# Loading the first expert's weights: four blocks at once, or two, one and two more

## The chip, the cores and the metric

One core of one Trainium2 chip runs the whole program in one launch. The metric is the device time of one execution in microseconds (us), median of the timed runs. The engines of the core are TensorE (PE: matmuls and transposes; its weight loads are listed as PEld), VectorE (DVE), ScalarE (ACT), GpSimd (POOL) and SyncE (SP), which here only issues transfers. Sixteen DMA engines move the data.

## The reference

Three stages: attention with a block-causal mask over 32 heads of 576 tokens, a mixture of eight experts in which each of the 2304 tokens goes to the expert with the highest logit, and a two-layer network with a piecewise quadratic activation.

```
scores = where(mask, q @ k.T / 8, -1e9); attn = softmax(scores); x = attn @ v   # B, H, S, D = 4, 8, 576, 64
x = x as [2304, 512]
logits = x @ w_gate + modality_bias[modality_id]
e_idx = argmax(logits); gate_w = softmax(logits)[e_idx]
for e in range(8):                       # w1[e]: 512 x 1024, w2[e]: 1024 x 512
    h = maximum(x[e_idx == e] @ w1[e], 0)
    out[e_idx == e] = gate_w * (h @ w2[e])
h = out @ w_in                           # 512 x 2048
g = where(h >= 1, h, where(h <= -1, 0, (h + 1)**2 / 4))
result = g @ w_out                       # 2048 x 512
```

All is float32. The kernel keeps the accuracy by splitting operands into a high and a low part and adding three products.

## The kernel before

The program runs through attention (to about 218 us), the experts (to about 446) and the network. Every engine works in an order that is written out by the program's text.

**Attention** goes through 16 pairs of heads, each in seven steps (`scores`, `flip`, `soft`). The rows of x of a finished batch are written to DRAM by `rows` (the store is line 459). From pair 14 on the generator `early` (`Routing.first_slot`) finds the expert that most of the first 13 row tiles go to; when it is done, `weights.begin` is called (line 519), still inside attention.

**The weights** of an expert come in eight blocks f = 0 to 7 of 128 hidden units. A block is 128 columns of w1 and 128 rows of w2, two transfers of 256 KB on SyncE's queue (lines 566 and 568). There are four buffers (`NRAW`). `Weights.load(most)` issues blocks, in order, until `most` are held in `self.raw`; a block leaves `raw` when `convert` has made its low part.

**The experts** run as five slots of 512 tokens; slots 0 and 1 are for the expert that was found first. `run_slots` goes over the blocks (s, f), numbered z. In each, `convert(s, f, 0)` lets ScalarE cast a raw block to its high part `wh` (line 1100) two blocks ahead, and `convert(s, f, 1)` lets VectorE make the low part `wl` (line 1103) one block ahead, which frees the raw buffer. `first` multiplies by w1 (line 1019) and takes ReLU on ScalarE to `hh` and on VectorE to `hl`; `second` multiplies by w2 (line 1128). `gather` fetches a slot's rows by indirect transfers on GpSimd (line 1078); `turn` transposes 128 rows, and ScalarE and VectorE split them into `xhi` and `xlo` (lines 76 and 77).

**The seam** is the generator `begin`, which still has attention's last work to do. Its order: casts of block 0, row group 0 turned, the rest of the last pair, row group 1 turned, cast of block 1, three of the left rows of x (`tail.rows`), and, at u == 3, `weights.load()` and a `yield`. Then the loop of `run_slots` begins with z = 0: cast of block 2, low part of block 1, `weights.load()`, and the first half (256 columns) of the first h. Between its halves `first` lets `begin` go on: row groups 2 and 3 are turned and the remaining left rows are made. The second half of the first h needs these two row groups.

So before the change four blocks are issued at `weights.begin`, block 4 at the seam, block 5 in z = 0, block 6 in z = 1 and so on.

Of the kernel before, what the change touches and what calls it, by code (L numbers as in the profile page):

```python
# [39 lines left out]
NFIRST = 2  # L40
# [3 lines left out]
NRAW = 4  # L44
# [78 lines left out]
def attention(late, weights, tc, q, k, v, ids, w_gate, mbias, x_dram, dram, ident, tabs):  # L123
# [15 lines left out]
    def load_pair(n, names="qkv"):  # L139
        b, c = divmod(n, NP)  # L140

        queue = dict(q=nc.sync if n else nc.scalar, k=nc.sync, v=nc.sync)
        for nm, src in zip("kqv", (k, q, v)):
            if nm not in names:
                continue
            dt = F32 if nm == "v" or n < COPY else F32R
            x = (pvp if nm == "v" else io).tile([P, 5, P], dt, tag=nm, name=f"{nm}{n}", bufs=3)
            if nm == "v":
                for h in range(2):
                    nc.sync.dma_start(  # L150
                        out=x[:, :4, h * D:(h + 1) * D],
                        in_=src[b, 2 * c + h, :512, :].rearrange("(t p) d -> p t d", p=P))

                for p0, s0 in ((0, 512), (64, 448)):
                    nc.sync.dma_start(
                        out=x[p0:p0 + 64, 4, :].rearrange("p (h d) -> p h d", d=D),
                        in_=src[b, 2 * c:2 * c + 2, s0:s0 + 64, :].rearrange("h p d -> p h d"))
            else:

                part = copies.pop((n, nm)) if n >= COPY else src[b, 2 * c:2 * c + 2]  # L160
                for h in range(2):
                    hs = slice(h * D, (h + 1) * D)
                    queue[nm].dma_start(out=x[:, :3, hs].bitcast(F32),
                                        in_=part[h, :384, :].rearrange("(t p) d -> p t d", p=P))
                    queue[nm].dma_start(out=x[:, 3:, hs].bitcast(F32),
                                        in_=part[h, 320:, :].rearrange("(t p) d -> p t d", p=P))
            io_t[n, nm] = x
# [4 lines left out]
    def copy_pair(n):  # L172

        b, c = divmod(n, NP)
        for nm, src in zip("kq", (k, q)):
            t = dram.tile([2, S, D], F32, name=f"{nm}c{n}")
            flat = "h s d -> (h s d)"
            nc.sync.dma_start(out=t.rearrange(flat).rearrange("(p x) -> p x", p=P),
                              in_=src[b, 2 * c:2 * c + 2].rearrange(flat).rearrange("(p x) -> p x", p=P))
            copies[n, nm] = t  # L180
# [124 lines left out]
    def scores(n, i):  # L305
        if n not in nmaxs:
            nmaxs[n] = wk.tile([P, NB], F32, tag="nmax", name=f"nmax{n}")
        j, heads = kinds[i]
        qa, qb, qf = qas[n % 2], qbs[n % 2], qfs[n % 2]
        kT, kd, kl = qk[n]  # L310
        if j == 4:

            pss = ps2.tile([P, 1024], F32, tag="big", name=f"s{n}_{i}")[:, 512 - S // 2:512 + S // 2]
            for c0, c1 in ((0, S // 2), (S // 2, S)):
                for z, (a, b) in enumerate(((qa[:, 0, 6:8], kd[:, 0]), (qzs[n % 2], kd[:, 1]), (qb[:, 6:8], kl))):
                    nc.tensor.matmul(pss[:, c0:c1], a, b[:, c0:c1], start=(z == 0), stop=(z == 2))
            return pss
        w = P * (j + 1)
        pss = ps1.tile([P, 512], F32, tag="s", name=f"s{n}_{i}", bufs=SB)[:, :w * len(heads)]
        for u, h in enumerate(heads):  # L320
            us = slice(u * w, (u + 1) * w)
            if j == 0:
                nc.tensor.matmul(pss[:, us], qf[:, h], kT[:, :w], start=(u == 0), stop=False)
            else:
                x = slice(2 * j - 2, 2 * j)
                nc.tensor.matmul(pss[:, us], qa[:, h, x], kd[:, h, :w], start=(u == 0), stop=False)
                nc.tensor.matmul(pss[:, us], qb[:, x.start + 8 * h:x.stop + 8 * h], kl[:, :w], start=False, stop=False)
        u = len(heads)
        nc.tensor.matmul(pss.rearrange("p (u w) -> p u w", u=u)[:, :, w - 64:], maskq,
                         maskk[:, :64 * u], start=False, stop=True)  # L330
        return pss
# [137 lines left out]
    def act(n, z, at):  # L469

        if n >= B * NP:
            return
        for what in PLAN.get((z, at), ()):
            if what == "q" and n + 1 < B * NP:
                load_q(n + 1)
            elif what == "k" and n + 1 < B * NP:
                load_k(n + 1)
            elif what == "rows" and todo:
                done.add(todo[0])
                rows(*todo.pop(0))  # L480
            elif n == 0:
                continue
            elif isinstance(what, tuple):
                weigh(n - 1, *what)
            elif what == "sum" and (n - 1) % 2:
                row_sums((n - 1) // NP, (n - 1) % NP // 2)
            elif what == "first":
                weigh_first(n - 1)
            elif what == "store":
                store_xT(n - 1)  # L490
                if (n - 1) % 2:
                    todo.extend((j, (n - 1) % NP // 2) for j in rows_of[(n - 1) // NP])
# [5 lines left out]
    for g in range(len(steps) + LAG):  # L498
        n, z = divmod(g, NK)
        if z in (0, 1) and n + 2 < B * NP:  # L500
            load_pair(n + 2, "v" if z else "qk")
        if z == 3 and COPY <= n + 4 < B * NP:
            copy_pair(n + 4)
        act(n, z, 0)
        pss = scores(*steps[g]) if g < len(steps) else None
        act(n, z, 1)
        later = flip(*steps[g - LAG]) if g >= LAG else []
        if pss is not None:
            soft(*steps[g], pss)
        for dst, src in later:  # L510
            nc.vector.tensor_copy(dst, src)  # L511
        if n >= B * NP:
            continue

        if n >= 14:
            assert all((j, a) in done for j in range(NEARLY) for a in range(2))
            for _ in range(EARLY[1] if weights.raw else EARLY[0]):
                if next(early, None):
                    weights.begin(0, range(1, NFIRST))
        act(n, z, 2)  # L520
        if (n, z) == (1, 0):
            load_gate()
        if (n, z) == (6, 0):
            routing.constants()
            early = routing.first_slot(ps1)
        if n == 8 and z == 5:
            routing.prep(ids, mbias, ident, ps1)
# [425 lines left out]
def experts_and_mlp(ctx, bctx, late, tc, a_tail, weights, w_in, w_out, x_dram, y_dram, g_dram, out,  # L953
# [111 lines left out]
    def run_slots(slots, begin, between, part=0):  # L1065
# [83 lines left out]
        for z, (s, f) in enumerate(blocks):  # L1149
            nxt = s + 1 if s + 1 in slots else None  # L1150
            if f == 1 and nxt:
                gather(nxt)
            if z + CONV < len(blocks):
                convert(*blocks[z + CONV], 0)
            between(s, f, 0)
            if z + CONV - 1 < len(blocks):
                convert(*blocks[z + CONV - 1], 1)
            weights.load()
            between(s, f, 1)
            if (s, f) == (NSTAT - 1, NF - 2) and not part:  # L1160
                tc.mark_branch_hint_location("more", engines=ENGINES)

            first(s, f)
            between(s, f, 2)
            if z > 0:
                second(*blocks[z - 1])
            if f in TURNS and nxt:
                turn(nxt, TURNS.index(f))
            between(s, f, 3)
# [3 lines left out]
    def begin(turn, convert):  # L1173
        tail.row_sums()
        convert(0, 0, 0)
        convert(0, 0, 1)
        turn(0, 0)
        tail.weigh()
        tail.weigh_first()
        tail.store_xT()  # L1180
        turn(0, 1, True)
        convert(0, 1, 0)
        for u, (j, a) in enumerate(tail.left):
            if u in (3, 4, 6):
                xr = b_y.tile([P, DM], F32, tag="y", name=f"xrows{u}")
            if u == 3:
                weights.load()
                yield
                turn(0, 2)
                turn(0, 3, True)  # L1190
            tail.rows(j, a, u % 3 == 0, None if u < 3 else xr[:, u % 2 * 256:(u % 2 + 1) * 256])
        tail.ps2.close()
        tail.pv.close()
        tabs.late_pool = late.enter_context(tc.tile_pool(name="r_late", bufs=1, side="right"))
        tabs.psa = pool("psa", 4, space=PSUM, side="right")
# [385 lines left out]
```

## Time and profile before

| | |
|---|---|
| median of 3 runs | 840.74 us (840.67 to 841.1) |
| the profiled execution | 839.69 us |
| its span, first to last instruction | 837.8 us |
| mean granted TensorE clock | 0.992 |
| busy: PE, DVE, ACT, POOL | 98%, 73%, 59%, 25% of the span |

Times in the trace count from the span's start. An idle time in square brackets stands before an instruction, with what ended it. A line xN stands for N instructions one behind the other; its second number is then the time from the first start to the last end. The granted clock is 1.00 at 2.4 GHz and 0.50 at 1.2 GHz. The DMA share is the mean busy share of the 16 DMA engines. Matmuls are pipelined, and their ends are modelled.

### The profile page before, as it was taken

To read this page: it belongs to the slowest core of one execution; us is meant where nothing else is said; L and a number is where in the kernel's file an instruction comes from. 1 tells how busy PE (TensorE), PEld (TensorE's weight loads), DVE (VectorE), ACT (ScalarE), POOL (GpSimd) and SP (SyncE) were. 2 spreads that over 40 slices of the span, in tenths; PEclk is the share of its full clock that TensorE was granted. 3 is DMA by queue.
4 is the path that set the end of the run, shared out by engine and by line. 5 is a ranking of instruction groups with operands and counts; after the bars stand their busy time and mean duration, and the time that the engine had idled before them with its cause. 6 is when DMAs were issued, how large, how long until landed. Compare 5 with 4: busy or idle time off the path is not lost. (4 is left out here: it accounts for less than half of the span.)

```text
span 837.8 us, 13997 instructions
## 1 busy us (share of the span) xinstructions
PE 817.9 (98%) x4936; PEld 709.3 (85%) x4936; DVE 608.3 (73%) x1115; ACT 495.6 (59%) x994; POOL 205.4 (25%) x249
## 2 busy tenths in 40 slices
PE   6999999998899999999999999999999999999998
PEld 5777777775788888888888999999999988888887
DVE  6788888789666656797873766766636877777774
ACT  5898888896533334464544666766657644444442
POOL 8546556546301212120202000110000011112120
PEclk6999999999999999999999999999999999999999
DMA  6445655630744447765625453453644633333301
GB/s 155 119 125 144 172 145 134 171 95 20 247 131 150 153 125 234 240 204 163 203 84 162 142 176 121 170 175 134 218 120 160 239 143 128 125 126 126 132 32 38
DMA packets 138058, 123.17 MB, mean 147 GB/s; under 512 B 70183, under 2 KB 122423, under 8 KB 135296
## 3 DMA queue, kind: packets, MB, share of 16 engines
q1 hardware_dynamic: 132256, 107.98, 41.9%
q0 software_dynamic: 4384, 13.92, 4.7%
q8 instruction: 40, 0.66, 0.3%
q10 hardware_dynamic: 1344, 0.33, 0.2%
q14 instruction: 34, 0.28, 0.1%
HBM read 89.17 MB, written 40.37 MB: 155 GB/s over the span
## 5 line engine op out<-in xcount | busy, mean ns | idle before, releaser
L1019 PE MATMUL h<-yhi,wi 128*128 128x384 f32 x768 | 200.4, 338 | 1.1 <-ACTq L1253 1.1
L1019 PEld LDWEIGHTS h<-yhi,wi 128*128 128x128 f32 x768 | 139.5, 188 | 1.5 <-ACTq L1253 1.5
L1019 PE MATMUL h<-ylo,wi 128*128 128x384 f32 x384 | 129.2, 337 | 0.0
L1293 ACT ACTIVATE cl<-h,half 128x384 f32<-128x384 f32 x96 | 55.9, 582 | 69.4 <-PE h L1019 69.1
L350 ACT ACTIVATE pall<-s,nmax 128x384 f32<-128x384 f32 (+2 forms) x144 | 79.5, 558 | 28.1 <-DVE nmax L344 17.0
L1297 DVE SCALAR_TENSOR_TENSOR gg<-cl,h 128x384 f32<-128x384 f32 x96 | 52.3, 552 | 51.8 <-ACT cl L1294 49.7
L1423 PE MATMUL p<-wo,s 128*128 128x256 f32 (+1 forms) x432 | 87.8, 338 | 0.0
L1423 PEld LDWEIGHTS p<-wo,s 128*128 128x128 f32 x432 | 68.5, 188 | 9.2
L1478 POOL DMA_INDIRECT out_dram<-rest,tab x16 | 27.3, 1707 | 190.9 <-DVE rest L1445 185.4
L1019 PEld LDWEIGHTS h<-ylo,wi 128*128 128x128 f32 x384 | 72.1, 188 | 0.0
L368 PE MATMUL pt<-ident,pall 128*128 128x128 f32 x400 | 65.7, 282 | 5.5 <-DVE pT L511 3.5
L1423 PE MATMUL p<-wo,a 128*128 128x256 f32 (+1 forms) x330 | 66.0, 335 | 0.0
L1019 PE MATMUL h<-xhi,wh 128*128 128x512 f32 (+2 forms) x164 | 63.1, 385 | 0.0
L1019 PE MATMUL h<-xhi,wl 128*128 128x512 f32 (+2 forms) x164 | 61.7, 376 | 0.5 <-DVE wl L1103 0.5
L1019 PE MATMUL h<-xlo,wh 128*128 128x512 f32 (+2 forms) x164 | 61.6, 376 | 0.0
L1128 PE MATMUL acc<-wh,hl 128*128 128x512 f32 x152 | 59.6, 392 | 0.1
L1423 PEld LDWEIGHTS p<-wo,a 128*128 128x128 f32 x330 | 52.8, 188 | 7.9
L1128 PE MATMUL acc<-wl,hh 128*128 128x512 f32 x152 | 59.3, 390 | 0.0
L1128 PE MATMUL acc<-wh,hh 128*128 128x512 f32 x152 | 59.1, 389 | 0.0
L393 PE MATMUL px<-pT,v 128*64 128x448 f32 (+4 forms) x320 | 54.5, 432 | 0.0
L1294 ACT ACTIVATE cl<-cl 128x384 f32<-128x384 f32 x96 | 50.5, 526 | 3.0
L368 PEld LDWEIGHTS pt<-ident,pall 128*128 128x128 f32 x400 | 43.9, 143 | 7.0 <-issue 3.1
(316 smaller groups left out, 1807.8 us busy)
## 6 DMA issues: line engine op xcount, KB each, us to landing
raw<-in_moe_w_dram SPq DMA_DIRECT2D x80, 256.0 KB
g_dram<-gg SPq DMA_DIRECT2D x48, 384.0 KB
g<-g_dram SPq DMA_DIRECT2D x18, 1024.0 KB
wi_raw<-in_moe_w_in_dram SPq DMA_DIRECT2D x16, 512.0 KB
wo_raw<-in_moe_w_out_dram SPq DMA_DIRECT2D x16, 512.0 KB
yr<-y_dram SPq DMA_DIRECT2D x18, 256.0 KB
x_dram<-xrow SPq DMA_DIRECT2D x33, 128.0 KB
v<-in_v_dram SPq DMA_DIRECT2D x32, 128.0 KB
```

The costliest lines, as they stand in the source:

```text
L350: nc.scalar.activation(pall[n % 2][:, o:o + w], pss[:, u:u + w], AF.Exp, bias=nm[:, x:x + 1], scale=1.0, accum_out=ssum[:, b, c, x:x + 1])
L368: nc.tensor.transpose(pt[:, kk, :], pa[:, o + kk * P:o + (kk + 1) * P], ident)
L393: nc.tensor.matmul(pxs[n][h * 64:(h + 1) * 64, s0 - 64:], io_t[n, "v"][:, kk, h * D:(h + 1) * D], pTs[n][:, kk, h, s0:], start=(kk == 0), ...
L1019: nc.tensor.matmul(ps, a[za], b[zb], start=(i == 0), stop=(i == n - 1))
L1128: nc.tensor.matmul(accs[s][u], a[:, us], b[:, 1, :], start=(f == 0 and i == 0), stop=(f == NF - 1 and i == 2))
L1293: nc.scalar.activation(cl, ph, AF.Relu, bias=half, scale=0.5)
L1294: nc.scalar.activation(cl, cl, AF.Square)
L1297: nc.vector.scalar_tensor_tensor(gg[:, :, f % 2, :], cl.rearrange(t3, t=P), 1.0, ph.rearrange(t3, t=P), op0=ALU.min, op1=ALU.max)
L1423: nc.tensor.matmul(o, a, b, start=(x == 0 and i in FRESH), stop=(x == len(terms) - 1), skip_group_check=True)
L1478: outs.append(nc.gpsimd.indirect_dma_start(out=out[:, :], out_offset=bass.IndirectOffsetOnAxis(ap=tabs.tab[:, j, 0:1].bitcast(U32), axis=0 ...
```

## The change

`weights.begin` loads two blocks instead of four. The load at the seam fills up to two held blocks; at that place block 0 has been released and block 1 has not, so it issues one block, block 2. The load in step z of the loop fills up to 3 + z blocks, at most four: in z = 0 blocks 3 and 4, in z = 1 blocks 5 and 6, and from z = 2 one block a step as before.

```diff
@@ -516,7 +516,7 @@
             for _ in range(EARLY[1] if weights.raw else EARLY[0]):
                 if next(early, None):
-                    weights.begin(0, range(1, NFIRST))
+                    weights.begin(0, range(1, NFIRST), 2)
         act(n, z, 2)
@@ -1155,7 +1155,7 @@
             if z + CONV - 1 < len(blocks):
                 convert(*blocks[z + CONV - 1], 1)
-            weights.load()
+            weights.load(min(NRAW, 3 + z))
             between(s, f, 1)
@@ -1184,7 +1184,7 @@
             if u == 3:
-                weights.load()
+                weights.load(2)
                 yield
```

`run_slots` serves further slots too, behind a branch; in the trace of before there are 40 blocks, five slots of eight, so that branch is not taken.

## Rows read from the trace of the kernel before

**Rows 1.** The page: span, busy time by engine, the chain that ended last.
```profile
span 837.8 us, 13997 instructions
...
PE 817.9 (98%) x4936; PEld 709.3 (85%) x4936; DVE 608.3 (73%) x1115; ACT 495.6 (59%) x994; POOL 205.4 (25%) x249
...
PE h L1019 24%; PE p L1423 21%; PE yt L1059 1%; PE p L1427 0%; DVE rest L1440 0%; DVEq L1440 0%
```

**Rows 2.** What PE waited for, 219 to 445: total us, times, longest.
```profile
PE h L1019 <- DVE wl L1103: 0.5, 2, 0.2
```

**Rows 3.** Busy us by engine in stretches of the seam; clock, DMA share, GB/s.
```profile
212.00:214.50 2.50, 2.50 (x27) 1.98 (x25) 0.55 (x3) 1.83 (x5) 1.89 (x3) 1.00 1.06 308
214.50:218.00 3.50, 0.93 (x6) 0.61 (x5) 1.73 (x4) 1.80 (x6) 1.14 (x2) 1.00 0.97 309
218.00:223.00 5.00, 4.84 (x39) 3.91 (x40) 3.47 (x11) 2.98 (x8) 0.94 (x1) 1.00 0.94 321
...
226.50:230.50 4.00, 3.99 (x31) 3.69 (x30) 3.02 (x9) 1.50 (x3) 1.98 (x2) 1.00 0.88 273
```

**Rows 4.** Timeline of PE at the stop: start, us, instruction [idle before it].
```profile
215.82 0.33 PE L368 MATMUL pt<-ident,pall 128*128 128x128 f32 x1 [1.22 <-issue]
...
218.13 0.84 PE L368 MATMUL pt<-ident,pall 128*128 128x128 f32 x6 [1.49 <-DVE pT L511]
```

**Rows 5.** Timeline of DVE at the stop.
```profile
215.24 0.43 DVE L344 TENSOR_REDUCE nmax<-s 128x2 f32<-128x256 f32 x1 [2.66 <-PE pt L368]
```

**Rows 6.** Timeline of SyncE's queue at the seam (the issues, not the transfers).
```profile
210.33 0.41 SPq L566 DMA_DIRECT2D raw<-in_moe_w_dram  x1
...
214.48 0.84 SPq L568 DMA_DIRECT2D raw<-in_moe_w_dram  x1
...
226.49 0.39 SPq L566 DMA_DIRECT2D raw<-in_moe_w_dram  x1
227.10 0.39 SPq L568 DMA_DIRECT2D raw<-in_moe_w_dram  x1
...
229.15 1.34 SPq L459 DMA_DIRECT2D x_dram<-xrows  x3
```

**Rows 7.** Timeline of ACT at the seam.
```profile
223.67 2.02 ACT L1100 CAST wh<-raw 128x1024 fp32r<-128x1024 f32 x2
226.49 1.07 ACT L76 CAST xhi<-xt 128x512 fp32r<-128x512 f32 x2 [0.80 <-PE xt L1093]
230.07 0.60 ACT L1116 ACTIVATE hh<-h 128x512 fp32r<-128x512 f32 x1 [2.50 <-PE h L1019]
230.56 1.04 ACT L1100 CAST wh<-raw 128x1024 fp32r<-128x1024 f32 x1
```

**Rows 8.** Timeline of PE: the second half of the first h, its first xlo product.
```profile
228.45 0.38 PE L1019 MATMUL h<-xlo,wh 128*128 128x256 f32 x1
```

**Rows 9.** Timeline of DVE: the low parts of row groups 2 and 3.
```profile
227.11 1.29 DVE L77 TENSOR_TENSOR xlo<-xt,xhi 128x512 fp32r<-128x512 f32 x2 [0.17 <-issue]
```

**Rows 10.** Timeline of SyncE's queue: a block's first issue, later in slot 0.
```profile
251.55 0.38 SPq L566 DMA_DIRECT2D raw<-in_moe_w_dram  x1
```

**Rows 11.** Stretches around that block; the last two numbers are DMA share, GB/s.
```profile
251.50:252.50 1.00, 1.00 (x7) 0.80 (x6) 1.00 (x2) 0.31 (x1) 0.00 (x0) 1.00 0.00 0
252.50:254.50 2.00, 2.00 (x13) 1.69 (x12) 1.46 (x3) 1.53 (x2) 0.00 (x0) 1.00 0.81 259
254.50:255.50 1.00, 1.00 (x6) 0.83 (x5) 0.84 (x1) 0.00 (x0) 0.00 (x0) 1.00 0.02 6
```

**Rows 12.** Stretches at the start of the run; the granted clock stands before DMA share.
```profile
5.00:10.00 5.00, 1.43 (x12) 1.22 (x12) 3.60 (x7) 2.99 (x7) 4.43 (x13) 0.77 0.71 154
10.00:15.00 5.00, 4.12 (x15) 3.00 (x16) 2.56 (x7) 2.74 (x8) 3.01 (x11) 0.50 0.62 141
...
20.00:25.00 5.00, 4.99 (x34) 3.98 (x34) 3.25 (x7) 4.42 (x15) 1.73 (x2) 0.86 0.84 221
```

**Rows 13.** Timeline of PE at the start of the run.
```profile
10.39 0.69 PE L326 MATMUL s<-kd,qa 128*128 128x384 f32 x1 [3.42 <-DVE qa L260]
```

## The prediction

> **What bounds the kernel now.** I read the page first: TensorE is busy 817.9 of 837.8 us, and the chain that ended last is TensorE alone from the start of the second layer to the end [rows 1]. So the run is one long string of matmuls, and what counts is how much TensorE idles. Next I read what TensorE waited for between the experts' start (219) and the second layer: 0.5 us in all [rows 2]. Every microsecond that TensorE loses at the seam (from attention to the experts, about 210 to 230) is therefore late at the end by its full length, and none can be caught up.
>
> Then the seam, first by stretches [rows 3]. TensorE works through 212 to 214.5, works only 0.93 of the 3.5 us from 214.5 to 218, and is full again behind that. The DMA engines are full (share 1.06, 0.97 and 0.94) from 212 to 223. The stop is two idle pieces of 1.22 and 1.49 us, 2.7 us together [rows 4]; VectorE idled 2.66 us before it too [rows 5]. The queue of SyncE [rows 6] shows what fills the DMA engines: eight transfers of 256 KB, the four blocks, issued from 210.33 to 214.48. The four gathers of the first slot's rows (128 rows of 512 floats, 256 KB each) go out in the same time. Together that is 3.1 MB, at the 309 GB/s of [rows 3] about 10.2 us, from 212 to 222: the length of the full stretch.
>
> **The change part by part.**
>
> *Two blocks instead of four when the expert is known.* It takes four issues and 1.05 MB out of the stretch from 212.6 to 215.3. On SyncE nothing follows from it, since its next work waits for VectorE anyway. What it may give is the stop of 2.7 us. No row names the cause of that stop: the engines wait for each other's signals while the DMA engines are full. Bounds: no gain (0) if it comes from something else, 2.7 if the flood is the cause and half of it would be harmless; a loss has no source here, since issues and bytes only go. But the flood is not gone in time: the first two blocks and the four gathers are still 2.1 MB, 6.8 us at 309 GB/s, from 212 to 218.8, so the DMA engines are as full through the whole stop as now. I take a gain of 0.7, a quarter.
>
> *One block at the seam.* The place in the program is that of today's seam load: SyncE issues it behind three stores of x rows, at 226.49 and 227.10 [rows 6]. Today it is block 4, which nobody wants for nine microseconds. Changed it is block 2, and ScalarE's cast of block 2 is the second of the two casts at 223.67 [rows 7], ahead of the load. That is the step that costs. ScalarE works in the order of the program: at 230.07 it idled 2.50 us for the matmuls of h before its hh, though the cast queued behind that (230.56) had its data long before [rows 7]. So behind the waiting cast stand the two xhi copies of row groups 2 and 3 (the pair at 226.49), then hh. For the xhi copies wait VectorE's two xlo [rows 9], for these the second half of the first h on TensorE (228.45, [rows 8]), and behind that in TensorE's order everything else.
>
> How long it takes: a block that has the DMA engines to itself is issued from 251.55 [rows 10]; its bytes (2.0 us at 259 GB/s, 518 KB) move from 252.5 to 254.5 [rows 11], that is 3.0 us from issue to the last byte. At the seam the stores and the next slot's gathers share the engines (share 0.88 over 226.5 to 230.5, [rows 3]). Lower end 3.0 us (landed at 229.5); upper end 4.0, when that busy stretch ends at 230.5. I take 3.4, landed at 229.9, nearer to the undisturbed block because this one stands first among the loads.
>
> From there by today's lengths: cast 1.0 (half of 2.02), xhi pair 1.07 [rows 7], and from the end of the xhi pair to the end of the xlo pair 228.40 - 227.56 = 0.84 [rows 9]. TensorE goes on at 229.9 + 2.9 = 232.8 instead of 228.45, where it came without a gap: 4.4 us lost, between 4.0 and 5.0 by the two ends. Nothing covers it: the transposes and row products ahead of that matmul are done by 228.4 and the next matmuls stand behind it.
>
> *Two a block until four are held.* Blocks 3 and 4 are issued right behind block 2, four issues where there were two, about 1.2 us more of SyncE ahead of the x row stores of 229.15 [rows 6]. Those stores wait for VectorE, which is 4.4 us late itself, so this costs nothing; without that cover, 1.2 us on a queue that TensorE does not wait for. Block 3 lands one or two microseconds behind block 2, and its cast stands behind hh, which is not before 234 then: in time. Block 5 goes out behind the late x row stores, about 235, and lands by 239; today its cast is at 241, then 245: hidden. From there the loads run as before. Bytes and issues of the whole run are the same.
>
> *The clock.* At the start of this trace TensorE idled 3.42 us before its matmul at 10.39 [rows 13]; the granted clock fell to half around then (0.77, then 0.50 in two stretches of 5 us, of which one stands, then 0.86, [rows 12]; that is 2.3 + 5 + 5 + 1.4 = 13.7 us at 1.2 GHz) and came back after TensorE had run its last few microseconds without a gap. The stop at 214.5 to 218, two pieces with work between, left it at 1.00 [rows 3]. The new stop is 4.4 us in one piece, longer than the one that cost the clock. So I count a fall. Price: 0 if it stays, and half of 13.7, 6.9 us, if it stays down as long as at the start. There TensorE had gaps; here it runs dense from 232.8, like the last stretch before the rise, so I take about 3.4 us at half, 1.7 us lost. The same shows the edge: a fall would cost more than all that the earlier part of the change can give.
> The Trainium skill (TensorE: Matmul & The Clock Gate, Part 1: The HAM clock gate) says that the default is the half clock and that sustained activity releases it. By it an idle wait for a DMA is paid twice, once as idle time and once as slow matmuls behind it, which is the rule that speaks against moving a load towards its use; rows 12 and 13 agree. Without the rule the sum would be 1.7 less.
>
> **Sum.** The profiled execution took 839.69 us (span 837.8 and 1.9 around it); the runs have a median of 840.74, 1.05 above. The change of time: - 0.7 + 4.4 + 1.7 = + 5.4. On the profiled execution 845.1, on the median 846.1, which I forecast.
>
> **Rivals.**
> 1. *The clock stays up.* For it: after the 2.7 us stop it did. Against it: one piece of 4.4 us. Then + 3.7: 844.4.
> 2. *The flood is the cause of the stop, and less of it suffices.* For it: the stop is the only one in this stretch and falls in the fullest part of the DMA engines, when the last of eight issues goes out. Against it: from 218 to 223 they are just as full and TensorE runs. Then - 2.7 + 4.4 = + 1.7, 842.4; with the clock's fall 844.1.
> 3. *Block 2 comes early enough that no one waits* (or something else makes its cast late anyway), and the stop stays: no change, 840.7. Against it: the issue stands behind stores whose rows are computed after 224, and the cast is due at 224.6.
> 4. *Faster*: the stop goes whole and the wait for block 2 costs less than it gives. The place is ScalarE's cast of block 2, the price 2.7 - w, where w is the wait that reaches TensorE. It decides at w = 2.7, that is a block landed within 1.7 us of its issue (4.4 goes with 3.4). At w = 0.5 it would be 838.5. Against it: alone on the DMA engines a block takes 3.0.
>
> **How the numbers follow.** Forecast (stop of 4.4 and the clock falls) 0.50, its own range 844 to 849; rival 1 0.25; rival 2 0.13; rival 3 0.06; rival 4 0.06. Measurements of this kernel tell 0.2%, 1.7 us, from no change: slower means above 842.4. The forecast, rival 1 and most of rival 2 lie there: 0.84. Same: rival 3 and a little of rivals 2 and 4, 0.09. Faster: 0.07. The range goes from 841.8 (rival 2 with the lower end of the wait, 4.0, is 842.0, and 0.2 for the measurement) to 849.2 (upper end of the wait, no gain, and some 7 us at half clock: 5.0 + 3.4); outside of it are rivals 3 and 4 and a long fall.
>
> **What would show it.** In the changed profile ScalarE idles over 4 us before its third cast of raw weights, ended by a DMA; TensorE shows one gap of 4 to 5 us between row products and the second half of the first h, and a stretch of 0.5 clock behind it. The two gaps at 214.6 and 216.6 are there, somewhat shorter. The forecast is wrong if the cast of block 2 starts without a wait, if that gap is under 2.7 us, or if TensorE is without gaps from 212 to 219.

## The result and the profile after

The changed kernel takes 845.39 us, median of 5 runs (844.94 to 846.17), against 840.74 before; the ratio is 1.0055, 95% interval 1.0041 to 1.0070. That is 4.65 us more. The forecast was 846.1 and slower. The profiled execution took 845.39 too, with a span of 843.3. The profiled execution of before lies 1.05 us under its median, so the two spans differ by 5.5.

The page of the changed kernel: TensorE has the same 4936 matmuls and 1.3 us more of busy time, in a span that is 5.5 us longer (compare [rows 1]).
```profile
span 843.3 us, 13998 instructions
...
PE 819.2 (97%) x4936; PEld 709.9 (84%) x4936; DVE 607.6 (72%) x1115; ACT 495.3 (59%) x994; POOL 204.7 (24%) x249
```
So it is mostly idle time, and the list of what TensorE waited for between 219 and 450 shows it (total us, times, longest). Beside the 0.5 us of [rows 2] there is now one wait of 4.0, put down to the xhi copies of ScalarE, 0.3 for the xlo behind them, and 0.5 for one hl.
```profile
PE h L1019 <- ACT xhi L76: 4.0, 1, 4.0
PE h L1019 <- DVE wl L1103: 0.5, 2, 0.2
PE acc L1128 <- DVE hl L1117: 0.5, 1, 0.5
PE h L1019 <- DVE xlo L77: 0.3, 1, 0.3
```
Why ScalarE is late is on its own timeline, which answers to [rows 7]:
```profile
222.35 1.07 ACT L1100 CAST wh<-raw 128x1024 fp32r<-128x1024 f32 x1
228.92 1.04 ACT L1100 CAST wh<-raw 128x1024 fp32r<-128x1024 f32 x1 [5.50 <-DMA raw<-in_moe_w_dram]
229.87 1.06 ACT L76 CAST xhi<-xt 128x512 fp32r<-128x512 f32 x2
...
235.07 1.04 ACT L1100 CAST wh<-raw 128x1024 fp32r<-128x1024 f32 x1
```
The two casts that stood together at 223.67 are now apart: the second, block 2, waits 5.50 us for its transfer, and the xhi pair goes 0.95 behind it. SyncE's queue (as [rows 6]) shows where the transfer comes from: behind the stores, at 225.13, with blocks 3 and 4 right behind it and the x row stores late at 232.12.
```profile
217.21 7.73 SPq L459 DMA_DIRECT2D x_dram<-xrow  x4
225.13 0.39 SPq L566 DMA_DIRECT2D raw<-in_moe_w_dram  x1
...
232.12 1.60 SPq L459 DMA_DIRECT2D x_dram<-xrows  x3
```
From the first issue of block 2 to its cast are 3.8 us. TensorE's timeline shows the stop (the two idle pieces of [rows 4], here 0.51 and 1.64), the gap (the new wait of 3.98 us at 227), and the slow matmuls behind it:
```profile
208.67 0.17 PE L723 MATMUL inv<-ohp,ohb 128*128 128x8 bf16 x1
...
214.35 0.33 PE L368 MATMUL pt<-ident,pall 128*128 128x128 f32 x1 [0.51 <-issue]
...
216.81 0.85 PE L368 MATMUL pt<-ident,pall 128*128 128x128 f32 x6 [1.64 <-DVE pT L511]
217.68 0.53 PE L1093 MATMUL xt<-identr,xg 128*128 128x128 f32 x4
...
230.99 0.58 PE L1019 MATMUL h<-xhi,wh 128*128 128x256 f32 x1 [3.98 <-ACT xhi L76]
231.82 0.58 PE L1019 MATMUL h<-xlo,wh 128*128 128x256 f32 x1 [0.26 <-DVE xlo L77]
...
234.34 0.63 PE L1019 MATMUL h<-xhi,wh 128*128 128x512 f32 x1
...
237.27 0.39 PE L1019 MATMUL h<-xhi,wh 128*128 128x512 f32 x1
...
237.95 0.39 PE L1128 MATMUL acc<-wh,hh 128*128 128x512 f32 x1
...
452.45 0.45 PE L1019 MATMUL h<-yhi,wi 128*128 128x384 f32 x1 [1.13 <-ACTq L1253]
```
The same matmul of 512 columns takes 0.63 at 234.34 and 0.39 at 237.27. The stretches of the changed kernel (busy us by engine, then the granted clock, DMA share and GB/s, as in [rows 3]) say why: the granted clock is at half from inside the gap on.
```profile
213.80:216.80 3.00, 0.86 (x6) 0.63 (x6) 1.52 (x4) 1.96 (x7) 1.05 (x2) 1.00 0.99 341
216.80:222.00 5.20, 5.17 (x42) 4.21 (x43) 3.34 (x11) 3.10 (x7) 0.96 (x2) 1.00 0.42 133
...
227.00:231.00 4.00, 0.02 (x2) 0.02 (x1) 0.52 (x1) 2.02 (x3) 0.69 (x1) 0.80 1.03 335
231.00:236.00 5.00, 4.74 (x16) 4.11 (x17) 2.85 (x10) 1.43 (x2) 0.00 (x0) 0.50 0.78 252
236.00:241.00 5.00, 5.00 (x31) 3.99 (x30) 4.52 (x10) 0.83 (x3) 0.00 (x0) 0.98 0.45 148
```
The kernel before has the same marks on TensorE's timeline at these times:
```profile
209.45 0.17 PE L723 MATMUL inv<-ohp,ohb 128*128 128x8 bf16 x1
...
219.00 0.53 PE L1093 MATMUL xt<-identr,xg 128*128 128x128 f32 x4
...
228.07 0.38 PE L1019 MATMUL h<-xhi,wh 128*128 128x256 f32 x1
...
232.61 0.39 PE L1128 MATMUL acc<-wh,hh 128*128 128x512 f32 x1
...
446.89 0.45 PE L1019 MATMUL h<-yhi,wi 128*128 128x384 f32 x1 [1.13 <-ACTq L1253]
```
Between the marks the time went here (us):

| stretch on TensorE | before | changed | difference |
|---|---|---|---|
| start to first inv matmul (before any change) | 209.45 | 208.67 | - 0.78 |
| inv to first xt transpose (the stop) | 9.55 | 9.01 | - 0.54 |
| xt to second half of the first h (the wait) | 9.07 | 13.31 | + 4.24 |
| second half to first acc matmul (the clock, and 0.26 of wait) | 4.54 | 6.96 | + 2.42 |
| first acc to the second layer | 214.28 | 214.50 | + 0.22 |
| second layer to the end | 390.9 | 390.9 | 0.0 |

### The profile page after: what moved, and what is told of

Same layout as the page of the kernel before. It is cut to its first block, busy times and chain, and to the rows that moved or that the text cites. A ratio compares the mean times of both kernels' runs of the same rounds, so it can differ in the third digit from the quotient of the medians.

```text
span 843.3 us, 13998 instructions
## 1 busy us (share of the span) xinstructions
PE 819.2 (97%) x4936; PEld 709.9 (84%) x4936; DVE 607.6 (72%) x1115; ACT 495.3 (59%) x994; POOL 204.7 (24%) x249
## 5 line engine op out<-in xcount | busy, mean ns | idle before, releaser
L1100 ACT CAST wh<-raw 128x1024 fp32r<-128x1024 f32 x40 | 41.9, 1048 | 18.8 <-PE acc L1128 13.2
```

The costliest lines, as they stand in the source:

```text
L1100: nc.scalar.copy(ws[s, f][0], weights.raw[s, f])
```

## The experiments

Each of the three sets ran on a chip of its own (8, 7 and 15) and on an occasion of its own, and the kernel before is not equally fast in them: 840.87, 836.98 and 837.18. The chip of the first comparison is not on record. Ratios are to before on the same chip. "xt to h" and "h to acc" are the third and fourth stretch of the table above.

**Three blocks early** (chip 8).
```diff
-                    weights.begin(0, range(1, NFIRST), 2)
+                    weights.begin(0, range(1, NFIRST), 3)
```


> Three blocks when the expert is known, none at the seam, the rest as changed. Theory: the loss is ScalarE's cast of block 2 waiting for its transfer (4.2 us of TensorE idle) and the half clock behind that (about 2.4). Then no TensorE gap over 0.3 us between 219 and 425, clock 1.00 there, 840.2 to 840.8. Rival, the loss comes from the later blocks being issued two at a time: a gap or waits behind 230 stay, 843 or more. Rival, half the flood is what matters for the stop at 214: the stop goes back from 2.15 to 2.7 us; if the stop has nothing to do with the bytes it stays at 2.1.


840.33 us, ratio 0.9992 (0.9984 to 1.0001). With block 2 early the two casts stand together again, and the xhi pair comes without a wait for a load:
```profile
223.63 2.02 ACT L1100 CAST wh<-raw 128x1024 fp32r<-128x1024 f32 x2
226.44 1.07 ACT L76 CAST xhi<-xt 128x512 fp32r<-128x512 f32 x2 [0.79 <-PE xt L1093]
```
The whole loss hangs on block 2; that blocks 3 and 4 go out together at the seam costs nothing. The stop was 0.49 + 1.61, not longer with the third block than with two. Behind the stop the clock fell, which I had not expected.

**The cast behind the matmuls** (chip 8). All loads as changed.
```diff
-            if z + CONV < len(blocks):
+            if z + CONV < len(blocks) and (s, f) != (0, 0):
                 convert(*blocks[z + CONV], 0)
...
             first(s, f)
+            if (s, f) == (0, 0):
+                convert(*blocks[z + CONV], 0)
```


> All loads as changed; only ScalarE's cast of block 2 stands behind the first h instead of ahead of it. Theory, ScalarE's order is what hands the wait on: block 2 still lands at the same time, but the xhi copies no longer stand behind it, no TensorE gap over 0.5 us after 219, clock 1.00, 840.2 (0.5 under before, by the shorter stop). Rival, TensorE itself or VectorE needs block 2 or the transfers slow everything at the seam: a gap of 2 us or more stays, 843 or more.


841.10 us, ratio 1.0006 (0.9993 to 1.0018). The 4 us gap is gone though the loads are as late as in the changed kernel: xhi no longer stands behind the cast. ScalarE's order was the carrier. But the expected time was missed by 0.9, and the profile has a new wait: the next cast, of block 3, waits 3.00 us for its load and starts 7.0 us after the first issue of it, with hh behind it; VectorE's routing work stands behind the hl that waits for this hh, and TensorE waits for the routing.
```profile
227.76 0.38 SPq L566 DMA_DIRECT2D raw<-in_moe_w_dram  x1
```
```profile
226.60 1.07 ACT L76 CAST xhi<-xt 128x512 fp32r<-128x512 f32 x2 [1.76 <-PE xt L1093]
...
234.72 1.05 ACT L1100 CAST wh<-raw 128x1024 fp32r<-128x1024 f32 x1 [3.00 <-DMA raw<-in_moe_w_dram]
235.67 0.59 ACT L1116 ACTIVATE hh<-h 128x512 fp32r<-128x512 f32 x1
```
```profile
237.15 0.27 PE L674 MATMUL rkp<-oh,ones 128*128 128x40 bf16 x5 [1.53 <-DVE oh L666]
```
In the changed kernel block 3 is issued at the same place behind block 2, and its cast comes only at 235.07, without a wait: the wait for block 2 hides it.

**Block 2 ahead of the stores** (chip 8, and once more on chip 15).
```diff
         convert(0, 0, 1)
+        weights.load(2)
         turn(0, 0)
...
             if u == 3:
-                weights.load(2)
                 yield
```


> Two blocks when the expert is known, block 2 issued at the head of the seam ahead of the three x row stores instead of behind them. Theory: issued about 217.6, landed about 221, cast at 223 without a wait, no gap, 840.2. Rival, a block at the seam is late wherever it is issued, since the gathers still fill the DMA engines: a wait of 1 us or more before the third cast, 842 or more.


839.10 us, ratio 0.9982 (0.9972 to 0.9992). Issued at 217.70, the block is there for the casts at 223.37, which stand together:
```profile
217.70 0.38 SPq L566 DMA_DIRECT2D raw<-in_moe_w_dram  x1
```
```profile
223.37 2.02 ACT L1100 CAST wh<-raw 128x1024 fp32r<-128x1024 f32 x2
```
On this chip it beat the kernel before. The clock had a surprise: it fell behind the stop (0.51 + 1.65 us here), as it did in the profiles of the two experiments above (0.49 + 1.61 and 0.49 + 1.60).
```profile
214.50:218.00 3.50, 1.85 (x12) 1.66 (x11) 2.67 (x9) 1.60 (x7) 0.61 (x1) 0.77 0.84 288
218.00:223.00 5.00, 5.00 (x37) 4.08 (x36) 2.20 (x5) 2.71 (x6) 0.94 (x1) 0.82 0.62 187
```

**The gap filled** (chip 8): as changed, and TensorE has small matmuls to do while it would idle.
```diff
                 next(opening, None)
+                if (s, f) == (0, 0) and a == 0:
+                    for _ in range(64):
+                        nc.tensor.matmul(ph[:, m // 2:m // 2 + P], routing.ones, routing.ones, start=True, stop=True)
```


> As changed, with 64 small bf16 matmuls (128 columns) queued on TensorE where it idles; they write columns that the next matmuls overwrite. Theory: the wait stays (TensorE takes up its own work at the same place, 4.2 us late), the fillers take 3.6 us of it, the granted clock stays 1.00, and the time is 845.4 - 2.4 = 843.0. Rival, the clock's fall costs little because other engines bound the stretch behind it: 845 or more. Rival, the clock falls all the same: 0.50 behind the gap and 845.4.


844.36 us, ratio 1.0048 (1.0034 to 1.0061). In the profile the theory holds: the fillers take 3.74 us, TensorE's own work comes back at 230.90 as late as in the changed kernel, and the clock stays up.
```profile
226.76 3.74 PE L1117 MATMUL h<-ones 128*128 128x128 bf16 x64
230.90 0.38 PE L1019 MATMUL h<-xhi,wh 128*128 128x256 f32 x1 [0.40 <-ACT xhi L76]
231.74 0.39 PE L1019 MATMUL h<-xlo,wh 128*128 128x256 f32 x1 [0.46 <-DVE xlo L77]
```
```profile
227.00:231.00 4.00, 3.60 (x64) 3.42 (x61) 0.61 (x1) 2.02 (x3) 0.61 (x1) 1.00 1.01 332
231.00:236.00 5.00, 4.54 (x25) 3.86 (x26) 3.88 (x14) 1.54 (x2) 0.00 (x0) 1.00 0.69 226
```
From h to acc it is 5.01 us, 0.46 of them idle, against 6.96 with the fallen clock, 0.26 of them idle: 1.95 us is the clock's price at this place, 2.15 if the idle time is taken out of both. The two spans differ by 1.6 (843.3 and 841.7). The medians do not show it: 844.36 is 1.4 above the 843.0 that I expected, and the ratio of 1.0048 is not clear of the changed kernel's 1.0055 (intervals 1.0034 to 1.0061 and 1.0041 to 1.0070). My sum had begun from the 845.4 of the first comparison, and the changed kernel was not run on chip 8, so what the filling gives in the time of a whole run stays open.

**One block early** (chip 7). Blocks 1 and 2 go ahead of the stores, with `weights.load(2)` placed as in the experiment "Block 2 ahead of the stores".
```diff
-                    weights.begin(0, range(1, NFIRST), 2)
+                    weights.begin(0, range(1, NFIRST), 1)
```


> One block when the expert is known, blocks 1 and 2 at the head of the seam ahead of the three x row stores. It asks what the stop at 214 to 217 hangs on. TensorE's two gaps there were 2.71 us with four blocks, 2.10 with three, 2.15 with two. Theory, the weights' bytes make it: with one block under 1.5 us, and about 838.4. Rival, it is the gathers or the chain of ScalarE and VectorE in attention's last steps: still 2.0 to 2.2, and 839.1 as with block 2 ahead of the stores. Block 1 is issued about 217.7 and cast at about 223, so no wait; if it does wait there, a gap of 1 to 2 us and 841.


838.42 us, ratio 1.0013 (1.0004 to 1.0022), slower. Block 1 is late, then block 2 (ScalarE's timeline), and TensorE idles 0.91 + 0.46 us before and inside the second half.
```profile
222.82 1.05 ACT L1100 CAST wh<-raw 128x1024 fp32r<-128x1024 f32 x1 [1.94 <-DMA raw<-in_moe_w_dram]
224.25 1.05 ACT L1100 CAST wh<-raw 128x1024 fp32r<-128x1024 f32 x1 [0.38 <-DMA raw<-in_moe_w_dram]
```
The stop was one gap of 0.40. That looked like the theory, until the kernel before was profiled on the same chip.

**The kernel before again** (chip 7).


> The kernel before once more, for a second profile of the stop. If four blocks make it longer than two, the two gaps are again 2.5 us or more together; if the 2.71 of the first profile was chance, 2.0 to 2.2. Three of the last four profiles had the clock at half for 3.4 us behind the stop: if that is a matter of chance it shows here or not, at about 1.7 us in the span.


836.85 us, one run. Neither of the two cases that I had named came: with all four blocks early the stop is one gap of 0.40 too, in DMA engines as full as in [rows 3].
```profile
215.06 0.85 PE L368 MATMUL pt<-ident,pall 128*128 128x128 f32 x6 [0.40 <-DVE pT L511]
215.93 0.53 PE L1093 MATMUL xt<-identr,xg 128*128 128x128 f32 x4
```
```profile
214.50:218.00 3.50, 3.08 (x20) 2.22 (x20) 2.51 (x11) 3.02 (x6) 1.83 (x2) 1.00 1.04 351
```
Four early blocks alone therefore don't make the stop. Its two gaps were there in all six profiles of the first comparison and chip 8, and in none of the eight of chips 7 and 15, with one, two or four blocks.

**Half of the gathers** (chip 7): as one block early, and the kernel leaves out the gathers of row groups 2 and 3 of the first slot (groups 0 and 1 stand for them):
```diff
+                if s == 0 and u > 1:
+                    rows[s, u] = rows[s, u - 2]
+                    continue
                 r = b_rows.tile([P, DM], F32R, tag="rows", name=f"xg{s}_{u}")
```


> As the kernel with one early block, and row groups 2 and 3 of the first slot are not gathered (groups 0 and 1 stand for them, so part of the experts' work is done on the wrong rows): 0.5 MB instead of 1.0 MB of gathers in the stretch of the stop. Theory, bytes of any kind make the stop: under 1.2 us. Rival, the chain of attention's last steps makes it: 2.0 to 2.2 in spite of a quarter of the bytes.


837.95 us, one run; the stop is one gap of 0.40. Beside the run above it tells nothing about bytes: on this chip there was no stop to take away.

**The changed kernel again** (chip 7).


> The changed kernel once more, for a second profile and for times on the same chip as the others. Theory: one TensorE gap of about 4 us at 227 behind the same wait of ScalarE, clock at half for 3 to 7 us behind it, 845.0 to 845.8. Rival, the first profile's gap was an accident: a gap under 3 us.


844.36 us, ratio 1.0083 (1.0069 to 1.0097). Third cast, gap and clock are as in the first profile (xt to h 13.19, h to acc 6.84; before on this chip 9.08 and 4.54). The stop is 0.40 here as well, but TensorE waits 0.80 for the slot's first gather behind it.
```profile
216.99 0.50 PE L1093 MATMUL xt<-identr,xg 128*128 128x128 f32 x4 [0.80 <-DMA xg<-x_dram,gidx]
...
230.18 0.58 PE L1019 MATMUL h<-xhi,wh 128*128 128x256 f32 x1 [4.08 <-ACT xhi L76]
```
So the change costs 7.4 us on this chip, where the kernel before has no stop, and 4.65 in the first comparison. The 7.3 us between the two spans here are + 0.29 up to the first inv matmul, + 0.77 from there to xt, + 4.11 for the wait, + 2.30 for the clock, and - 0.17 behind it.

**The parts alone, and block 2 ahead again** (chip 15). The first part alone is `weights.begin(0, range(1, NFIRST), 2)` with the other two loads as before; the other parts alone are `weights.load(min(NRAW, 3 + z))` and `weights.load(2)` with four blocks at begin.

> Only the first part of the change: two blocks at begin; the other loads fill up to four as before, so the seam issues blocks 2, 3 and 4. Theory, this part alone makes the loss: ScalarE's third cast waits 5 us for its DMA, a gap of about 4 us, half clock behind it, 5 to 7.4 us over before. Rival, the limits on the later loads are needed for the loss (their issues stand ahead of the x row stores): under 3 us over before.


843.54 us, ratio 1.0074 (1.0060 to 1.0088): the first part alone is the loss. Its third cast:
```profile
227.20 1.04 ACT L1100 CAST wh<-raw 128x1024 fp32r<-128x1024 f32 x1 [5.56 <-DMA raw<-in_moe_w_dram]
```
From xt to h it takes 13.37, from h to acc 6.45.

> Only the other two parts: four blocks at begin, nothing at the seam, one block in the first step and two in the second. Theory: no cast waits, no gap, within 0.1% of before. Rival, block 4 a step later is late as well: a wait before the fifth cast and 1 us or more over before.


837.39 us, ratio 1.0000 (0.9991 to 1.0009): they do nothing, as expected.

> The kernel before, for a profile on the same chip as the other three. Theory, the stop belongs to the chip: its two gaps are as long as those of the other three kernels here within 0.4 us. Rival, it depends on the blocks: longer here and in the kernel with four early blocks than in the two with two.


837.9 us, one run. The first of the two gaps is 0.40 in all four kernels here. Behind it, ahead of the first transpose, TensorE waits again: with four blocks early 0.47 for the first gather in the kernel before and 1.66 with the other parts alone, with two blocks early 0.76 with block 2 ahead of the stores and nothing with the first part alone. So neither of the two cases that I had named came whole: the sums of the gaps differ by more than 0.4, and the kernel before has less than one of the two with two blocks. The profile puts the 1.66 down to a wh cast of ScalarE, but the transposes don't read it, and before they started at 216.84 while that cast ran from 216.89 on; I take it for the gather again, which is not shown.
```profile
216.84 0.50 PE L1093 MATMUL xt<-identr,xg 128*128 128x128 f32 x4 [0.47 <-DMA xg<-x_dram,gidx]
```
```profile
217.87 0.50 PE L1093 MATMUL xt<-identr,xg 128*128 128x128 f32 x4 [1.66 <-ACT wh L1100]
```


> Two early, block 2 ahead of the three x row stores, once more on another occasion. Theory, the seam costs nothing in this form and the stop at 214 to 217 belongs to the chip and not to the blocks: from the first slot's first transpose to the first acc matmul 13.6 to 14.4 us as before, the time within 0.2% of before if the chip shows no stop in the kernel before, and 0.2% under it at most where it does. Rival, fewer early blocks give the 1.8 us of the first comparison everywhere: 0.9982 of before again.


836.84 us, ratio 0.9996 (0.9987 to 1.0005); xt to h and h to acc are 8.84 and 4.55, as before. The gain of chip 8 did not come again where there is no stop. So block 2 ahead of the stores undoes the loss, and that it beats the kernel before is shown on one chip of two.

## Why the prediction was right, and where it was not

**What bounds the kernel**: right. What TensorE lost at the seam, 5.3 us at the first acc, is 5.6 at the second layer and 5.5 at the end.

**Block 2 at the seam**: right, in place, order and size. Forecast 4.4, measured 4.24 to the first matmul of the second half, and 0.26 more idle before the second, the xlo product that the forecast goes by: 4.5. Its pieces: from issue to cast 3.8 (taken 3.4, bounds 3.0 and 4.0), from cast to the xlo matmul 231.82 - 228.92 = 2.90 (worked out 2.9). On the other chips xt to h grew by 4.11 (chip 7), and 4.5 for the first part alone (chip 15). Three early blocks, the cast moved behind and the load moved ahead each take this term away, and the first part alone brings it, so its cause is shown: the transfer of block 2, handed to TensorE by ScalarE's order.

**Two a block until four are held**: right that it costs nothing. What I had not seen is that block 3 is late as well. I had it land one or two microseconds behind block 2; with the cast moved behind, it is cast 7.0 us after its issue, and TensorE idles 1.5 us for it. "In time" was true only behind the wait for block 2.

**The clock**: right that it falls; it did so in all three profiles that have the gap unfilled (3.98, 4.08 and 4.03 us). The reason given for it does not hold as it stands: that one long piece costs the clock and two pieces with work between do not. In three profiles on chip 8 it fell behind the two pieces of the stop. The size was taken too small: 3.4 us at half clock, where 4 x 0.40 + 5 x 1.00 + 5 x 0.04 = 6.8 were measured (shares below 1.00 twice over, from the three stretches from 227 on), 5.2 of them behind the gap. The term was 1.7, measured 2.42 - 0.26 = 2.2; with the gap filled 1.95 of the stretch went. The Trainium skill (TensorE: Matmul & The Clock Gate, Part 1: The HAM clock gate) has the half clock as the default that activity releases; the trace agrees, with a granted clock of 0.50 from 231 to 236 and 0.98 from 236 to 241, after TensorE had taken up its work again, and with 0.63 against 0.39 us for one form of matmul some 3 us apart.

**The stop**: the term that failed, though its number came out near (forecast - 0.7, first pair - 0.54); that is luck. I had taken a quarter of 2.7 as the yield of fewer bytes. Four early blocks go without the two gaps on two chips, so the bytes alone don't make them, and fewer of them gave nothing sure there. On chip 7 the changed kernel took 0.77 longer than before from inv to its first transpose, as much as its wait for a gather (0.80), although I had written that a loss has no source there; on chip 15 the two kernels with two blocks took 7.03 and 7.77, the two with four 7.48 and 8.68. Whether fewer blocks shorten the stop on a chip that has one is open. The first pair bears on it, one profile each, and the 1.8 us by which block 2 ahead of the stores beat the kernel before on chip 8, where the kernel before was not profiled.

**A term that no one forecast**: - 0.78 before anything is changed. The clock came back earlier at the start of the changed kernel's profile (0.59, 0.72 and 1.00 where [rows 12] have 0.50, 0.50 and 0.86). I take it for scatter of the start. The forecast of + 5.4 against + 5.5 of the two spans is thus closer than its parts: wait and clock measured 6.7 where 6.1 was forecast, and the - 0.78 made up for it. The medians differ by 4.65 in the first comparison and by 7.4 on chip 7, so that 846.1 came out within 0.7 us of the measured time is in part luck. What holds in all three profiles is the sum of wait and clock: 6.7, 6.4 on chip 7, and 6.4 for the first part alone on chip 15.

## What to carry to other kernels

Before a load is moved towards its use, look at what stands behind the instruction that will wait for it, on that engine: here a cast whose result was wanted 7 us later (in the kernel before it ends at 225.69, and VectorE takes it up at 232.68) stopped copies that were wanted at once. A wait that idles TensorE for some microseconds is to be priced with the clock behind it, here 4.5 and 2.2. And a stall seen in one profile may belong to the chip or the occasion; profile the same kernel on a second one before a change is credited with it.

## What the runs showed of the hardware that was not expected

One kernel differed by 3.9 us between chips (840.87 on chip 8 and 836.98 on chip 7). The stop can hold some of it: in the three profiles of the kernel before, inv to the first xt takes 9.55 us in the first comparison, 7.04 on chip 7 and 7.48 on chip 15. The two gaps sum to 2.09 to 2.71 us in six profiles; in the eight others there is one of 0.40, in four of them with a further wait of 0.47 to 1.66 ahead of the first transpose. Where the stop is, VectorE starts late: its first nmax begins 0.5 to 2.0 us after the last matmul of the scores that it reads (in the first profile of before that matmul, on line 329, ends at 213.07 + 0.22 = 213.29 and nmax begins at 215.24; the 2.66 of [rows 5] is all of VectorE's idle time). In the eight others that is at most 0.04, as in the kernel before on chip 7 (212.52 + 0.22 = 212.74 to 212.78):
```profile
212.78 0.43 DVE L344 TENSOR_REDUCE nmax<-s 128x2 f32<-128x256 f32 x1 [0.74 <-PE s L329]
```
The DMA engines are full in both of these profiles (share 0.97 in [rows 3], 1.04 on chip 7). No run here shows why, and since each set has a chip and an occasion of its own, the two can't be told apart.

The clock does not go by the length of a gap alone: it stayed at 1.00 behind gaps of 1.22 and 1.49 and of 0.51 and 1.64, and fell behind 0.51 and 1.65 in another execution.
